# Two key chunks per running-maximum step, and nine chunks of exponentials summed on GpSimd, in an attention and soft-MoE kernel

## The chip, the cores and the metric

The kernel runs on one core of a Trainium2 chip. The metric is the device time of one execution in microseconds (us), as the median of several runs. In what follows PE is TensorE's matrix multiplication, DVE is VectorE, ACT is ScalarE, POOL is GpSimd and SP is the queue of SyncE, which issues the loads and stores.

## The reference

Attention over pooled queries, and a soft mixture of experts on its output. All is float32; the sums over keys below are the part that the change touches.

```python
# q, k, v: (8 batches, 8 heads, 1152, 64); phi: (512, 32); w1: (8, 512, 1024); w2: (8, 1024, 512)
q_pool = q.reshape(B, H, S // 2, 2, D).mean(axis=3)          # 576 queries
scores = scale * np.matmul(q_pool, k.transpose(0, 1, 3, 2))  # 576 x 1152
scores = scores - np.max(scores, axis=-1, keepdims=True)
attn = np.exp(scores)
attn = attn / (np.sum(attn, axis=-1, keepdims=True) + 1e-09)
x = heads side by side of np.matmul(attn, v)                 # (4608, 512)
logits = x @ phi                                             # (4608, 32)
d = softmax of logits over all 4608 rows
slot_input = d.T @ x                                         # 32 slots, 4 for each of 8 experts
slot_out = np.maximum(slot_input[e] @ w1[e], 0) @ w2[e]
return softmax of logits over the 32 slots @ slot_out
```

## The kernel before

The attention is cut into 32 pairs of heads and each pair into three thirds of 192 pooled queries: 96 units, which run one after the other through a pipeline of several units' depth. A unit holds keys on the partitions: nine chunks of 128 keys, each a block of 128 partitions x (2 heads x 192 queries = 384 columns).

What a unit does, under the names that the order and the profile use:

- `S`: PE makes the scores of one or two chunks in a PSUM tile `sc` (two such tiles in turn; five tiles a unit, of chunks 0-1, 2-3, 4-5, 6-7 and 8). `C`: ACT copies the tile to the unit's SBUF buffer `s` (three buffers, so a unit's copy needs what was read of the unit three before). `X`: DVE takes the running maximum over chunks into `M`, reading the scores from PSUM, after ACT has read them.
- `mt`, `mc`, `mb`: PE turns `M` round, DVE reduces over keys, and PE spreads the maximum of each query over the partitions of a PSUM bank `m`. `sub`: DVE subtracts it from `s` in place, three chunks (1152 columns) at a time. `exp`: ACT takes the exponential of three chunks in place.
- `av`: PE multiplies the nine chunks by the values into `U`. `add`: POOL adds chunks up into `cs`. `sums`: PE multiplies `cs`, and what chunk POOL left out, by a matrix of ones, which sums over the keys. `zt`, `rc`, `rr`: DVE, ACT and DVE turn the sums into reciprocals; `xT`: POOL multiplies the unit's result by them. `qs`: POOL adds the query pairs of the next pair of heads, once in three units.

After each batch (12 units) the soft-MoE steps follow (`lg`, `to`, `cb`, `rm`, `nm`, `ex`, `cz`, `on`, `ga` and so on), mixed in among the units of later batches; the expert weights' products form the last 60 us.

Nothing is looped on the chip. `graph` lists all steps with a cost and a due time from the table `K["t"]`, `plan` takes them one by one and picks, on the engine that is free first, the ready step with the lowest due time, and the steps are written in that order. Each engine then runs its own list strictly in order, so a step that waits holds up all behind it on its engine. All engines' instructions go through the helper at L341, so in the profile the groups are told apart by tile names.

The nine chunks' sum is taken in two ways: `adds=(7, 7, 2)` says that POOL adds chunks 0 to 7 into one `cs`, seven additions each of which reads what the last one wrote, and `sums` lets PE take chunk 8 by itself and then `cs`. The last unit has two POOL additions and three on DVE into a tile `c2`. `maxi` makes one instruction for each chunk from 1 on: the first compares chunk 1 in PSUM with chunk 0 in `s`, the others compare a chunk in PSUM with `M`.

Of the kernel before, what the change touches and what calls it, by code (L numbers as in the profile page):

```python
# [9 lines left out]
F32 = mybir.dt.float32  # L10
# [15 lines left out]
    wait=dict(PE=0.086, ACT=0.046, DVE=0.0, Pool=4.872),  # L26
    adds=(7, 7, 2),
# [4 lines left out]
        S=(-419.409, -572.597, -228.216, -358.029, -359.095),  # L32
        C=(-84.784, 269.944, 218.068, -577.589, -79.03),
        X=(-761.046, -254.853, -1002.385, -608.138, -1071.065),
        mt=(-274.632,),
        mc=(-400.52,),
        mb=(-445.98,),
        sub=(-970.04, -736.195, 46.605),
        exp=(-298.507, -391.891, 8.919),
        add=(61.121, 79.596, 138.735, -61.814, 27.096, -118.037, -447.03, 87.051, -331.16),  # L40
        av=(-72.896, -655.1, 1.867, 139.969, 198.999, -251.069, -106.455, 238.404, 113.064),
        sums=(-46.238, -107.59, 249.379, -104.045, -13.513, -134.769, -185.84, -434.517, -83.5, -69.249),
        ue=(-426.57,),
        tc=(-460.765,),
        eps=(13.909,),
        rcp=(38.892,),
        tr=(4.372,),
        ad2=(92.766, -165.96, -728.717, -41.076, -40.387, 11.096, 31.403, 182.215, -386.141),
        nx=(-269.644,),
        ldk=(-344.296,),  # L50
        ldq=(349.768,),
        ldv=(-14.581,),
        qs=(107.426,),
        lg=(-279.404, -0.679, -381.845, 154.224),
        to=(560.808, 859.479, 646.063, 506.384),
        cb=(-186.311, 159.143),
        rm=(512.075, 120.581),
        nm=(-132.399,),
        ex=(-28.039,),
        ns=(400.668,),  # L60
        ce=(-460.62,),
        cz=(-13.045,),
        cm=(-565.973,),
        on=(574.955, 668.981, 964.928, 547.585, 762.85, 285.43, 526.881, 86.153, 107.36, 223.665, 295.103, 920.683),
        we=(-328.071, -289.113),
        ga=(20.378, -479.397, -578.354),
        end_lg=(106.83, -231.5, 354.048, 498.579),
        end_to=(-4.744, 972.49, 123.821, -202.665),
        end_cb=(-233.64, -225.948),
        end_rm=(374.475, 5.169),  # L70
        end_nm=(-356.522,),
        end_ex=(101.789,),
        end_ns=(202.856,),
        end_ce=(17.199,),
        end_cz=(89.883,),
        end_cm=(-72.978,),
        end_on=(262.546, 297.303, 519.604, 283.168, 921.932, -138.51, 416.415, -107.54),
        end_we=(-1262.411, -855.42),
        end_ga=(-16.24, -915.587, 124.689),
        fin_lg=(-453.425, -361.783),  # L80
        fin_to=(184.025, 13.836),
        fin_cb=(89.484, 234.863),
        fin_rm=(1078.782,),
        fin_nm=(-92.156,),
        fin_ex=(447.138,),
        fin_ns=(828.836,),
        fin_ce=(-538.17,),
        fin_cz=(-1160.965,),
        fin_cm=(-294.828,),
        fin_on=(676.225, 510.466, -82.377, 963.76),  # L90
        fin_we=(-453.209, -1047.033),
        fin_ga=(502.969, -358.259, 8.644),
        fin_gs=(-253.634,),
# [19 lines left out]
def pool_t(n):  # L113
    return 0.1 + 0.00241 * n, 0.06 + 0.00241 * n
# [8 lines left out]
def graph(K, B, HP, NT3, Q, NW):  # L123
# [223 lines left out]
def pooled_attention_soft_moe(ctx: ExitStack, tc: tile.TileContext, q, k, v, phi, w1, w2, out):  # L347
# [147 lines left out]
    class Unit:  # L495
# [458 lines left out]
```

## Time and profile before

| what | value |
|---|---|
| median of 3 runs | 993.19 us (992.81 to 994.21) |
| the profiled execution's own time | 993.46 us |
| its span, first to last instruction | 991.7 us |
| mean granted TensorE clock | 0.995 |
| busy share of the span: PE, DVE, POOL, ACT | 97%, 92%, 77%, 76% |
| first and last of the 96 first additions on POOL (`cs<-s`), start | 21.1 us, 916.7 us |

The profile gives, for each engine, the time in which it had an instruction in hand; PE's is modelled, since its matrix products overlap. Two instructions of one engine may overlap in the record by some tens of nanoseconds, so what an instruction costs its engine is read from start to start and not from its own length. The attention takes the span up to about 920 us and the expert products the rest; the argument is about the first.

### The profile page before, as it was taken

How to read it: one execution, taken by the hardware profiler on the slowest of the kernel's cores; microseconds unless marked ns; L12 is line 12 of the kernel's file. 1: busy time of each engine (PE TensorE's matmuls, PEld its weight loads, DVE VectorE, ACT ScalarE, POOL GpSimd, SP SyncE). 2: the span in 40 equal slices, each digit the busy share in tenths (PEclk: the TensorE clock that was granted, in tenths of full speed). 3: DMA queues.
4: the chain of work that ended last, by engine and by line, in shares of the span. 5: the costliest groups of instructions: out<-in, count | busy, mean ns of one | idle time of the engine just before them, and what ended most of it. 6: DMA issues, size and time to landing. Idle time of an engine off the chain costs nothing.

```text
span 991.7 us, 24308 instructions
## 1 busy us (share of the span) xinstructions
PE 958.6 (97%) x9358; PEld 673.0 (68%) x9358; DVE 910.1 (92%) x1595; ACT 753.9 (76%) x1120; POOL 768.4 (77%) x814
## 2 busy tenths in 40 slices
PE   6999999999999999999999999999999999999995
PEld 4666767677767777676677767777677777776542
DVE  5999999999999999999999999999999999999423
ACT  4778888787878788788778878787887888787323
POOL 2888888788888889888888888788897888888200
PEclk9999999999999999999999999999999999999998
DMA  5122322232242322212221211212221211213998
GB/s 170 49 92 94 115 94 94 70 104 82 70 140 70 115 92 73 95 58 104 73 82 63 69 53 52 71 49 73 73 73 52 70 49 54 68 47 131 345 405 351
DMA packets 27683, 101.24 MB, mean 102 GB/s; under 512 B 3504, under 2 KB 4016, under 8 KB 27568
## 3 DMA queue, kind: packets, MB, share of 16 engines
q1 hardware_dynamic: 27568, 99.69, 29.2%
q8 instruction: 74, 1.21, 0.5%
q14 instruction: 41, 0.34, 0.1%
HBM read 90.24 MB, written 9.44 MB: 101 GB/s over the span
## 4 chain that ended last, share of the span: by engine, by line
PE 51%; DVE 30%; issue 11%; ACT 5%; DMA 1%; SPq 0%; POOL 0%; ACTq 0%; DVEq 0%
PE sc L341 18%; DVE M L341 17%; PE U L341 15%; PE m L341 13%; DVE s L341 9%; PE b L341 5%; ACT s L341 5%; DVE rr L341 1%; DMA q<-in_q_dram 1%; DVE rmax L341 1%; DVE mc L341 1%; DVE bm L341 0%; DVE rc L341 0%; PE idle L341 0%; ACT lT L341 0%
## 5 line engine op out<-in xcount | busy, mean ns | idle before, releaser
L341 POOL TENSOR_TENSOR cs<-cs,s 128x384 f32<-128x384 f32 x571 | 573.1, 1004 | 54.7 <-ACT s L341 20.6
L341 ACT COPY s<-sc 128x768 f32<-128x768 f32 (+1 forms) x480 | 342.4, 737 | 145.9 <-PE sc L341 130.5
L341 PE MATMUL sc<-qs,k 64*128 64x192 f32 x3456 | 382.2, 347 | 20.9 <-DVE M L341 8.4
L341 DVE TENSOR_TENSOR s<-s,m 128x1152 f32<-128x1152 f32 x288 | 382.0, 1341 | 6.7 <-PE m L341 5.8
L341 DVE TENSOR_TENSOR M<-sc,M 128x384 f32<-128x384 f32 x672 | 367.7, 547 | 15.5 <-ACT s L341 4.8
L341 PEld LDWEIGHTS sc<-qs,k 64*128 64x128 f32 x3456 | 277.2, 188 | 122.9 <-issue 70.1
L341 PE MATMUL U<-s,v 128*64 128x192 f32 x3456 | 343.3, 331 | 0.2 <-ACT Us L341 0.2
L341 ACT ACTIVATE s<-s 128x1152 f32<-128x1152 f32 x288 | 333.0, 1169 | 13.0 <-DVE s L341 8.5
L341 PEld LDWEIGHTS U<-s,v 128*64 128x64 f32 x3456 | 234.1, 137 | 57.9 <-issue 26.7
L341 POOL TENSOR_TENSOR cs<-s 128x384 f32<-128x384 f32 x96 | 96.5, 1005 | 82.6 <-ACT s L341 81.8
L341 POOL TENSOR_TENSOR xT<-rr,Us 128x192 f32<-128x192 f32 x95 | 56.8, 598 | 2.8 <-DVE rr L341 2.7
L341 DVE TENSOR_TENSOR M<-sc,s 128x384 f32<-128x384 f32 x96 | 51.6, 538 | 5.0 <-ACT s L341 4.8
L341 POOL TENSOR_TENSOR qs<-q 128x576 f32<-128x576 f32 x31 | 44.0, 1419 | 13.9 <-DMA q<-in_q_dram 13.9
L341 DVE TENSOR_REDUCE mc<-m 128x3 f32<-128x384 f32 x96 | 52.4, 546 | 1.2 <-PE m L341 1.1
L341 PE MATMUL m<-ident,M 128*128 128x128 f32 x288 | 52.5, 291 | 0.0
L341 PE MATMUL m<-s,ones 128*64 128x192 f32 x388 | 52.5, 349 | 0.0
L341 PE MATMUL m<-ident,mc 128*128 128x128 f32 x288 | 51.1, 287 | 0.0
L341 PE MATMUL m<-cs,ones 128*64 128x192 f32 x384 | 49.7, 337 | 0.0
L341 PEld LDWEIGHTS m<-ident,M 128*128 128x128 f32 x288 | 29.8, 141 | 23.1 <-issue 22.8
L341 PEld LDWEIGHTS m<-ident,mc 128*128 128x128 f32 x288 | 29.9, 136 | 19.9 <-issue 12.2
L341 DVE STREAM_TRANSPOSE zt<-m 128x192 f32<-128x192 f32 x96 | 35.8, 373 | 1.1 <-PE m L341 1.1
L341 DVE STREAM_TRANSPOSE rr<-rc 128x192 f32<-128x192 f32 x96 | 35.4, 368 | 0.3
(90 smaller groups left out, 449.0 us busy)
## 6 DMA issues: line engine op xcount, KB each, us to landing
w<-in_moe_w_dram SPq DMA_DIRECT2D x64, 512.0 KB, 5.9
v<-in_v_dram SPq DMA_DIRECT2D x32, 576.0 KB, 3.8
k<-in_k_dram SPq DMA_DIRECT2D x31, 576.0 KB, 3.8
q<-in_q_dram SPq DMA_DIRECT2D x31, 576.0 KB, 3.8
out_dram<-ob SPq DMA_DIRECT2D x24, 384.0 KB, 4.2
q<-in_q_dram SPq DMA_DIRECT2D x1, 384.0 KB, 7.2
k<-in_k_dram SPq DMA_DIRECT2D x1, 320.0 KB, 5.7
k<-in_k_dram SPq DMA_DIRECT2D x1, 256.0 KB, 3.1
```

The lines of the kernel that those rows point to most:

```text
L341: return self.tc.keep_in_program_order(op(*args, **kwargs))
```

## The change

1. **Maximum over two chunks at a time.** `M` becomes two blocks of 384 columns. `X` of the tile of chunks 2-3 compares both with chunks 0-1 in `s` (768 columns, one instruction), the tiles 4-5 and 6-7 compare with `M` in the same way, a new step `Xf` (method `fold`) takes the maximum of the two blocks of `M`, both in SBUF, and chunk 8 is compared with the result. The tile of chunks 0-1 is no longer read by DVE. `M` has one buffer of twice the size in place of two.
2. **All nine chunks summed on POOL.** Eight additions in two sums: `cs` takes chunks 0, 1, 4, 6, 8, and chunk 2 takes 3, 5, 7 in place; the eighth addition puts chunk 2 onto `cs`. PE's `sums` has `cs` alone, in all but the last unit.
3. **Three small DVE instructions** that had a constant as operand (`nm`, the addition in `cz`, the addition before `zs`) get a second tensor in SBUF in its place.
4. **A new table of due times,** some step costs, and a term `stay` in `plan`, which favours a PE step that uses PE in the same mode (rows, columns or the full array) as the one before.

```diff
-    adds=(7, 7, 2),
+    stay=287.389,
+    adds=(8, 8, 2),
...
-        X=(-761.046, -254.853, -1002.385, -608.138, -1071.065),
+        X=(-718.744, -1124.601, -586.904, -1071.804, 795.214),
+        Xf=(-611.616,),
...
-        return ("add", u, max(c, 1)) if max(c, 1) <= adds[u] else ("sums", u, NC if c == 0 else c)
+        return ("add", u, (1, 1, 8, 2, 3, 4, 5, 6, 7)[c])
...
+        for i in range(1, na + 1):
+            if i == 1:
+                d = [("exp", u, 0), old(u > 1, "sums", u - 2, NC)]
+            elif na == 8:
+                d = [("add", u, i - 1 if i == 8 else max(i - 2, 1))] + [("add", u, 6) if i == 8 else ("exp", u, group_of[i + 1])]
+                d += [("av", u, 2)] if i == 2 else []
+            else:
+                d = [("add", u, i - 1), ("exp", u, group_of[i])]
...
-            k = min((k for k in ks if when[k] <= t0 + K["wait"].get(e, 0.0) + 1e-9), key=lambda k: (ops[k][2], at[k]))
+            k = min((k for k in ks if when[k] <= t0 + K["wait"].get(e, 0.0) + 1e-9),
+                    key=lambda k: (ops[k][2] - (K["stay"] if ops[k][7] == last and ops[k][7] else 0.0), at[k]))
...
         def maxi(self, i):
-            for x, c in enumerate(TI[i]):
-                if c:
-                    M = self.M
-                    if M is None:
-                        self.M = un.tile([P, 2, QU], F32, name=f"M{self.u}", tag="M")
-                        M = self.s[:, 0]
-                    dve.tensor_tensor(self.M, self.ps[i][:, :, x * QU:(x + 1) * QU], M, op=ALU.max)
+            if i == 1:
+                self.M = un.tile([P, 2, 2, QU], F32, name=f"M{self.u}", tag="M", bufs=1)
+            n = len(TI[i])
+            ps = self.ps[i][:, :, :n * QU].rearrange("p h (c q) -> p c h q", c=n)
+            if n == 2:
+                dve.tensor_tensor(self.M, ps, self.s[:, 0:2] if i == 1 else self.M, op=ALU.max)
+            else:
+                dve.tensor_tensor(self.M[:, 0], ps[:, 0], self.M[:, 0], op=ALU.max)
+
+        def fold(self):
+            dve.tensor_tensor(self.M[:, 0], self.M[:, 0], self.M[:, 1], op=ALU.max)
...
-        def add(self, c):
-            sv = self.s[:, c]
-            if c == 1:
+        def add(self, i):
+
+            s = self.s
+            if i == 1:
                 self.cs = un.tile([P, 2, QU], F32, name=f"cs{self.u}", tag="cs")
-            pool.tensor_tensor(self.cs, self.s[:, 0] if c == 1 else self.cs, sv, op=ALU.add)
+            if i == 1:
+                t = self.cs, s[:, 0], s[:, 1]
+            elif self.u == NU3 * B * HP - 1:
+                t = self.cs, self.cs, s[:, i]
+            elif i == 8:
+                t = self.cs, self.cs, s[:, 2]
+            elif i % 2:
+                t = self.cs, self.cs, s[:, i + 1]
+            else:
+                t = s[:, 2], s[:, 2], s[:, i + 1]
+            pool.tensor_tensor(*t, op=ALU.add)
...
-            dve.tensor_scalar(self.nm, new, -1.0, None, op0=ALU.mult)
+            dve.tensor_tensor(self.nm, zero, new, op=ALU.subtract)
...
-            dve.tensor_scalar(self.cz, self.cz, EPS, None, op0=ALU.add)
+            dve.tensor_tensor(self.cz, self.cz, eps[:NQ].to_broadcast([NQ, self.nt]), op=ALU.add)
...
-        dve.tensor_scalar(zs, rsum, EPS, None, op0=ALU.add)
+        dve.tensor_tensor(zs, rsum, eps, op=ALU.add)
```

What the new order does is shown at two places in the middle of the program. First DVE before, from the first maximum of unit 46 to its last (a row names the engine's operation, the tile written and the tiles read; the number behind a letter is the unit or buffer, and x2 stands for two alike in a row):

```order
L341 TENSOR_TENSOR M46_4497<-sc0_136,s1_139 128x384
L341 TENSOR_REDUCE mc45_4502<-m2_135 128x3
L341 TENSOR_TENSOR M46_4497<-sc1_137,M46_4497 128x384 x2
L341 TENSOR_TENSOR s0_138<-s0_138,m2_135 128x1152 x2
L341 TENSOR_TENSOR M46_4497<-sc0_136,M46_4497 128x384 x2
L341 STREAM_TRANSPOSE zt44_4559<-m0_133 128x192
L341 TENSOR_TENSOR M46_4497<-sc1_137,M46_4497 128x384 x2
L341 STREAM_TRANSPOSE rr43_4571<-rc43_4483 128x192
L341 RECIPROCAL rc44_4565<-rc44_4565 128x6
L341 TENSOR_TENSOR M46_4497<-sc0_136,M46_4497 128x384
```

Eight instructions write `M46`, six of them in pairs in which the second reads what the first wrote; `zt` and `rr` of units two and three back stand between them. The same stretch of DVE after the change, at unit 49:

```order
L350 TENSOR_TENSOR M49_4594<-sc0_138,s1_141 128x768
L350 TENSOR_TENSOR s0_140<-s0_140,m0_135 128x1152
L350 TENSOR_TENSOR M49_4594<-sc1_139,M49_4594 128x768
L350 TENSOR_TENSOR s0_140<-s0_140,m0_135 128x1152
L350 TENSOR_TENSOR M49_4594<-sc0_138,M49_4594 128x768
L350 STREAM_TRANSPOSE zt46_4650<-m2_137 128x192
L350 TENSOR_TENSOR M49_4594<-M49_4594 128x384
L350 RECIPROCAL rc46_4659<-rc46_4659 128x6
L350 TENSOR_TENSOR M49_4594<-sc1_139,M49_4594 128x384
L350 STREAM_TRANSPOSE rr46_4670<-rc46_4659 128x192
```

Five instructions write `M49`, no two of them next to each other; the fourth is the fold, which reads no PSUM. `zt` is now that of the unit three back. POOL before, over the additions of unit 46 and the first of unit 47:

```order
L341 TENSOR_TENSOR cs46_4649<-s1_139 128x384
L341 TENSOR_TENSOR cs46_4649<-cs46_4649,s1_139 128x384 x5
L341 TENSOR_TENSOR xT3_3837<-rr45_4718,Us45_4711 128x192
L341 TENSOR_TENSOR cs46_4649<-cs46_4649,s1_139 128x384
L341 TENSOR_TENSOR cs47_4745<-s2_140 128x384
```

There are seven additions in one chain, broken once by `xT`. POOL after the change, over the additions of unit 45 and the first of unit 46:

```order
L350 TENSOR_TENSOR cs45_4416<-s0_140 128x384
L350 TENSOR_TENSOR cs45_4416<-cs45_4416,s0_140 128x384 x2
L350 TENSOR_TENSOR s0_140<-s0_140 128x384 x2
L350 TENSOR_TENSOR cs45_4416<-cs45_4416,s0_140 128x384
L350 TENSOR_TENSOR s0_140<-s0_140 128x384
L350 TENSOR_TENSOR cs45_4416<-cs45_4416,s0_140 128x384
L350 TENSOR_TENSOR xT3_3738<-rr44_4486,Us44_4422 128x192
L350 TENSOR_TENSOR cs46_4503<-s1_141 128x384
```

There are eight additions, and the two sums take turns, in most units without a break but for the last two: over the whole program 2.5 additions a unit directly follow one that they depend on (125 `cs` behind the same `cs`, 32 chunk-2 sums behind the same sum, 80 last additions behind the chunk-2 sum that they read, over 96 units).

More of the change, by code (lines that the diff above doesn't have):

```diff
@@ L25 @@
     bufs=3,
-    wait=dict(PE=0.086, ACT=0.046, DVE=0.0, Pool=4.872),
-    adds=(7, 7, 2),
+    stay=287.389,
+    wait=dict(PE=0.226, ACT=0.162, DVE=0.177, Pool=0.222),
+    adds=(8, 8, 2),
     more=3,
@@ new lines @@
+        Xf=(-611.616,),
+        mt=(-723.921,),
+        mc=(-114.844,),
+        mb=(-258.845,),
+        sub=(-619.663, -102.814, 1329.497),
+        exp=(-642.998, 884.145, 2721.12),
+        add=(-198.042, 1322.564, -125.887, -190.614, 154.697, -76.997, 1064.624, 181.041, -383.843),
+        av=(-131.033, -285.378, 7.096, -154.967, -134.833, 1122.981, 753.574, 1255.771, 50.287),
+        sums=(248.993, -468.15, 1008.625, -343.84, -281.108, -244.636, -433.554, 1772.701, -715.422, 357.278),
@@ new lines @@
+        ue=(219.326,),
+        tc=(-619.755,),
+        eps=(-475.199,),
+        rcp=(587.085,),
+        tr=(1037.822,),
+        ad2=(-53.911, -555.751, -604.838, -526.867, 730.457, -438.819, -56.242, -328.898, -440.675),
+        nx=(-394.76,),
+        ldk=(1741.983,),
+        ldq=(-545.242,),
+        ldv=(-712.945,),
+        qs=(1280.303,),
+        lg=(444.851, 1827.585, 1378.479, 269.315),
+        to=(-352.527, -351.216, 595.522, -21.759),
+        cb=(-404.16, -621.947),
+        rm=(-593.4, -101.797),
@@ new lines @@
+        nm=(1924.0,),
+        ex=(868.118,),
+        ns=(1829.478,),
+        ce=(-122.558,),
+        cz=(2775.066,),
+        cm=(1393.56,),
+        on=(-454.454, -58.618, 1350.106, -112.696, 801.818, -835.286, 715.879, 207.384, 682.139, 1275.364,
+            -383.737, 661.371),
+        we=(-597.411, 350.652),
+        ga=(1799.669, -165.502, -420.515),
+        end_lg=(-98.197, -419.284, -79.663, -540.569),
+        end_to=(-608.902, -43.815, 408.079, 74.295),
+        end_cb=(513.126, -242.586),
@@ new lines @@
+        end_rm=(-231.148, 1919.33),
+        end_nm=(-65.218,),
+        end_ex=(-95.024,),
+        end_ns=(-432.945,),
+        end_ce=(-436.159,),
+        end_cz=(438.218,),
+        end_cm=(-559.666,),
+        end_on=(18.047, 1709.155, 1820.299, 6.308, 1328.871, -126.235, -611.963, 497.934),
+        end_we=(-367.952, -647.455),
+        end_ga=(-134.148, -375.889, -728.043),
+        fin_lg=(305.033, 82.614),
+        fin_to=(236.995, -870.323),
+        fin_cb=(236.963, -750.654),
+        fin_rm=(-13.239,),
@@ L94 @@
+        fin_nm=(-865.594,),
+        fin_ex=(-154.868,),
+        fin_ns=(478.151,),
+        fin_ce=(16.679,),
+        fin_cz=(1089.035,),
+        fin_cm=(-70.505,),
+        fin_on=(-1089.827, -542.03, 2626.542, 835.695),
+        fin_we=(-352.114, 782.849),
+        fin_ga=(-127.911, -315.564, -577.207),
+        fin_gs=(-350.135,),
     ),
@@ L187, in graph @@
             op(("C", u, i), "ACT", act_t(2 * Q * len(tl)), d)
-            m = sum(1 for c in tl if c)
-            if m:
-                d = [("C", u, i)] + ([("X", u, i - 1)] if i and (i > 1 or len(TI[0]) > 1) else [])
-                d += [old(u > 1, "mt", u - 2)] if c - m < 1 else []
-                t = dve_t(2 * Q)
-                op(("X", u, i), "DVE", (m * t[0], (m - 1) * t[0] + t[1]), d)
+            if i:
+                before = ("X", u, i - 1) if 1 < i < len(TI) - 1 else ("C", u, 0) if i == 1 else ("Xf", u)
+                op(("X", u, i), "DVE", dve_t(2 * Q * len(tl)), [("C", u, i), before] + [old(u and i == 1, "mt", u - 1)])
+            if i == len(TI) - 2:
+                op(("Xf", u), "DVE", dve_t(2 * Q), [("X", u, i)])
         b = ("m", u)
         op(("mt", u), "PE", 0.33, [("X", u, len(TI) - 1)], b, take=True)
-        op(("mc", u), "DVE", (0.485, 0.56), [("mt", u), old(u > 1, "mb", u - 2)], b)
+        op(("mc", u), "DVE", (0.465, 0.55), [("mt", u), old(u > 1, "mb", u - 2)], b)
         op(("mb", u), "PE", 0.34, [("mc", u)], b)
@@ L379, in pooled_attention_soft_moe @@
     nc.gpsimd.memset(eps, EPS)
+    zero = const.tile([P, 1], F32, name="zero")
+    nc.gpsimd.memset(zero, 0.0)
     ones = const.tile([P, D], F32, name="ones")
```

90 lines of the change are left out of this document (15 added, 75 removed).

## Prediction

> **What bounds the kernel now.** I read the page's busy shares, then one window of 770 us from the steady middle, then the groups of instructions in it, and last the timelines of DVE and POOL, for what one instruction costs from start to start.
>
> ```profile
> span 991.7 us, 24308 instructions
> core 0: us, PE busy (x) PEld busy (x) DVE busy (x) ACT busy (x) POOL busy (x), PEclk, DMA share, GB/s
> 110.00:880.00 770.00, 761.94 (x7440) 544.83 (x7438) 750.54 (x1294) 621.24 (x913) 653.00 (x685) 1.00 0.24 77
> L341 POOL TENSOR_TENSOR cs<-s x96: 990/1005/1017, 21.1 to 916.7; 128x384 f32<-128x384 f32 x96
> PE 51%; DVE 30%; issue 11%; ACT 5%; DMA 1%; SPq 0%; POOL 0%; ACTq 0%; DVEq 0%
> ```
>
> The first additions of units 0 and 95 start 895.6 us apart, so a unit takes 895.6 / 95 = 9.43 us. DVE is busy in 750.5 of 770 us, which is 9.19 us of each unit: it is the bound. PE looks as full, and half of the chain of waits is PE's, but its busy time is modelled and holds gaps like these:
>
> ```profile
> PEld m L341 <- issue: 62.8, 265, 0.5
> PEld sc L341 <- issue: 55.9, 206, 0.8
> PEld U L341 <- issue: 22.8, 115, 0.5
> 441.60 0.55 PE L341 MATMUL m<-s,ones 128*64 128x192 f32 x4
> ```
>
> In that window PE's weight loads stood idle for 141 us without a named cause, mostly where PE goes from one kind of product to another. I take PE as second, with slack. POOL's 653 us leave out the pauses inside its chains, which the next part adds.
>
> **Cost on DVE.** Before, a unit has eight maxima: two alone and three pairs.
>
> ```profile
> 447.75 0.54 DVE L341 TENSOR_TENSOR M<-sc,s 128x384 f32<-128x384 f32 x1
> 448.22 0.54 DVE L341 TENSOR_REDUCE mc<-m 128x3 f32<-128x384 f32 x1
> ...
> 451.44 1.14 DVE L341 TENSOR_TENSOR M<-sc,M 128x384 f32<-128x384 f32 x2
> 452.50 1.34 DVE L341 TENSOR_TENSOR s<-s,m 128x1152 f32<-128x1152 f32 x1
> 453.76 0.74 DVE L341 SCALAR_TENSOR_TENSOR slot<-slot,corr,m 96x512 f32<-96x512 f32 x1
> ```
>
> One alone takes 448.22 - 447.75 = 0.47 us, a pair 452.50 - 451.44 = 1.06 us, since its second waits for the first's result. A unit pays 2 x 0.47 + 3 x 1.06 = 4.12 us. The subtraction of 1152 columns takes 453.76 - 452.50 = 1.26 us, so 384 columns more cost (1.26 - 0.47) / 2 = 0.40 us, and a maximum over 768 columns, which no row has, about 0.87 us. (Its bounds are the pair's 1.06 and the 0.79 that the columns alone cost; I take the line through both lengths.) After: 3 x 0.87 + 0.47 for chunk 8 + a fold of 0.47 = 3.55 us. Clean, DVE saves 0.57 us a unit and falls to 8.62.
>
> But the fold reads two tensors in SBUF, as no other large instruction of the steady part does; the maxima and subtractions have one operand in PSUM. The trace has that form at the end, and small ones at each batch:
>
> ```profile
> 917.83 1.00 POOL L341 TENSOR_TENSOR cs<-cs,s 128x384 f32<-128x384 f32 x1
> 918.21 1.04 DVE L341 TENSOR_TENSOR c<-s 128x384 f32<-128x384 f32 x1
> 919.28 1.22 DVE L341 TENSOR_TENSOR c<-c,s 128x384 f32<-128x384 f32 x2
> 174.81 1.00 POOL L341 TENSOR_TENSOR cs<-cs,s 128x384 f32<-128x384 f32 x1
> 174.83 1.00 DVE L341 TENSOR_TENSOR rmax<-bm 128x1 f32<-128x1 f32 x1
> L341 DVE SCALAR_TENSOR_TENSOR rmax<-bm,rmax x7: 219/986/994, 288.5 to 925.6; 128x1 f32<-128x1 f32 x7
> L341 DVE SCALAR_TENSOR_TENSOR rsum<-rsum,corr,bs x8: 175/178/216, 308.5 to 931.3; 128x1 f32<-128x1 f32 x8
> L341 DVE TENSOR_SCALAR nm<-rmax x9: 153/154/155, 175.9 to 927.8; 128x1 f32<-128x1 f32 x9
> L341 DVE TENSOR_SCALAR cz<-cz x9: 164/166/169, 181.7 to 929.9; 96x6 f32<-96x6 f32 x7, 96x4 f32<-96x4 f32 x1, 96x2 f32<-96x2 f32 x1
> L341 DVE TENSOR_TENSOR M<-sc,M x672: 511/552/560, 8.5 to 911.0; 128x384 f32<-128x384 f32 x168
> ```
>
> The exact shape of the fold took 1.04 us beside a POOL addition and 0.56 without. It ended at 919.25, 0.42 us after POOL's addition ended at 918.83, and 384 columns cost 0.40 us: it did nothing until POOL was done. `rmax`, one column wide, took 0.99 us beside an addition of 1.00. `M`, with one operand in PSUM, never took over 0.56 us, though POOL was nearly always busy. So the fold costs what is left of POOL's instruction plus 0.42 us. POOL starts an addition about every 0.96 us (next part); if the fold meets it anywhere, 0.48 us are left on average, and the fold takes 0.90 us, that is 0.34 more than 0.56. Its bounds are 0.56 and 0.96 + 0.42 = 1.38 us.
>
> The new `nm` and the addition in `cz` have two SBUF inputs too. `nm` stands right behind `rmax`, when POOL has just begun its next addition: 0.15 becomes about 1.0 us as in `rmax`; `cz` gains about half an addition, 0.45. That is 1.3 us in 12 units, 0.11 each (bounds 0 and 0.16). The edit before `zs` runs once and can wait for one POOL instruction, 1.0 us at most, which I leave to the range. DVE: 9.19 - 0.57 + 0.34 + 0.11 = 9.07 us a unit.
>
> **Cost on POOL.**
>
> ```profile
> 441.48 1.01 POOL L341 TENSOR_TENSOR cs<-cs,s 128x384 f32<-128x384 f32 x1
> 442.44 1.42 POOL L341 TENSOR_TENSOR qs<-q 128x576 f32<-128x576 f32 x1
> 443.82 1.01 POOL L341 TENSOR_TENSOR cs<-s 128x384 f32<-128x384 f32 x1
> 444.90 1.00 POOL L341 TENSOR_TENSOR cs<-cs,s 128x384 f32<-128x384 f32 x1
> 445.88 0.59 POOL L341 TENSOR_TENSOR xT<-rr,Us 128x192 f32<-128x192 f32 x1
> 446.43 4.25 POOL L341 TENSOR_TENSOR cs<-cs,s 128x384 f32<-128x384 f32 x4
> 450.65 0.59 POOL L341 TENSOR_TENSOR xT<-rr,Us 128x192 f32<-128x192 f32 x1
> L341 POOL TENSOR_TENSOR cN<-cN,cz 96x192 f32<-96x192 f32 x7 | 3.5, 507 | 2.4 <-DVE cz L341 2.4
> ```
>
> An addition followed by something independent takes 442.44 - 441.48 = 0.96 us, one followed by an addition that reads its result 444.90 - 443.82 = 1.08: 0.12 for each dependent step. `qs` takes 1.38, a third of it, 0.46, on each unit; `xT` 0.55; `cN` 0.5 in 12 units, 0.04. Before: 7 x 0.96 + 4.9 dependent steps x 0.12 + 0.55 + 0.46 + 0.04 = 8.36 us, and POOL waits for the rest of 9.43. After: 8 x 0.96 + 2.5 x 0.12 + 0.55 + 0.46 + 0.04 = 9.03. The ninth chunk costs POOL 0.67 us, and it is nearly full.
>
> Then comes the fold seen from POOL. No row shows a POOL instruction behind a long DVE instruction of this form. Its bounds are 0, if POOL goes on beside it, and 0.56 us, the fold's whole length; I take 0.42, the time for which the fold ran alone after POOL's end. That gives 9.03 + 0.42 = 9.45 us a unit, 0.02 more than now. POOL becomes the bound.
>
> The Trainium skill, "SBUF — State Buffer", section "SBUF: two separate sides", states that a VectorE instruction with two SBUF inputs and a GpSimd instruction that reads SBUF hold their shared port pair exclusively for the whole instruction, and that the loser fully blocks. The rows of `c<-s` and `rmax` agree for VectorE as the loser; no row here shows GpSimd as the loser. Read literally, with the whole 0.56 us, it would make POOL 9.59 us a unit, an estimate.
>
> **What else moves.** PE loses one product with ones (four instructions, 0.55 us with its change of mode), and the new order changes PE's mode 64 times less; both fall on an engine with slack, and if POOL and DVE cover it, they bring nothing. The tile of chunks 0-1 is freed one maximum earlier and `M` has one buffer, not two: the first maximum of a unit must wait until PE has turned the last unit's `M`, but `mc` of that unit stands before it on DVE anyway. The in-place sum makes a unit's second tile copy wait for the eighth addition of three units before; that is over 14 us after its exponentials begin (two units of 9.4 less some 4.5 us for the first subtraction and exponential), and POOL needs 9.5, so POOL may lag 5 us before ACT waits. SP's list is the same but for some neighbours exchanged. The expert part at the end stays as it is.
>
> **The sum.** POOL's work sets the date of the last unit:
>
> ```profile
> 21.13 1.01 POOL L341 TENSOR_TENSOR cs<-s 128x384 f32<-128x384 f32 x1 [4.04 <-ACT s L341]
> 30.86 1.01 POOL L341 TENSOR_TENSOR cs<-s 128x384 f32<-128x384 f32 x1 [2.25 <-ACT s L341]
> ```
>
> From 21.1 us, 95 units at 9.45 and about 2 us in which POOL still waits for its second unit make 920.9 us, against 916.7: 4.2 us later. The last steps follow it as now. The profiled execution took 993.46 us, 1.8 more than its span and 0.3 more than the median of 993.19; so 993.5 + 4.2 = 997.7, as a median about 998 us. With the fold's price on POOL at 0.38 it would be 994, at 0.56 about 1011.
>
> **Rivals.** First, POOL is not held up, or for a short time only, since its own start-up runs under the fold. DVE's 9.07 us with today's idle 0.24, and POOL's 9.03, then give 9.25 to 9.31 us a unit, some 12 to 17 us less: about 978. For it speaks that no row shows POOL waiting; it decides as soon as POOL's loss is under 0.25 us a fold. Second, the folds mostly miss POOL's additions, or read without waiting: DVE at 8.62, POOL at 9.03, a unit near 9.15, 27 us less: 966. For it speaks `rsum`, whose two tensors lie in SBUF as well and which took 0.18 us at all eight batches: it came in a pause of POOL. Against it: every `rmax` and `c` that began beside a running POOL instruction waited, and with POOL nearly full there are few pauses. Third, the two effects cancel within 0.2%: POOL's loss is 0.35 to 0.4 us. Fourth, it is worse: POOL's loss is the whole 0.56, or its lag reaches `zt`, which waits in DVE's list for the sums; 1006 and more.
>
> **Chances.** About 0.2%, some 2 us, is what a measurement here can tell from no change. POOL-bound and slower, 995.2 to 1006: 0.37, the likeliest, predicted at 998. Worse than that: 0.09. Within 0.2%: 0.15. First rival, 970 to 991: 0.27; second, 955 to 970: 0.12. So faster 0.39, same 0.15, slower 0.46. The likeliest case's own range is 995 to 1006; to hold 8 in 10 with both signs I give 964 to 1009, which leaves out part of the second rival and of the worst case.
>
> **What would show it.** In the profile after: `M<-sc,M` of 768 columns near 0.94 us long; the fold `M<-M` near 0.9 us on average and seldom 0.55; POOL's start-to-start of independent additions 0.96 us, with longer ones, near 1.4, where a fold ran; POOL's waits for `exp` gone and DVE's idle grown to some 0.4 us a unit; `nm` near 1.0 us. If POOL still waits for ACT, or its additions beside a fold are no longer than others, the first rival holds. If the folds take 0.55 us, the second does.

## The result, and the profile after

| | before | after |
|---|---|---|
| median | 993.34 us (992.81 to 994.21, 4 runs) | 1017.58 us (1016.49 to 1019.08, 4 runs) |
| ratio | | 1.0244 (95%: 1.0226 to 1.0262) |
| profiled execution, its span | 993.46, 991.7 us | 1016.49, 1014.5 us |
| granted TensorE clock | 0.995 | 0.994 |

The changed kernel is 2.4% slower. The direction was forecast, the size was not: 1017.6 lies above the range. Two rows of the page after, the span and the shares of the chain of waits; then the window of 770 us (the columns are those of the row of before), the first additions on POOL, and what PE waited for in that window (in all, times, longest):

```profile
span 1014.5 us, 23218 instructions
...
DVE 36%; PE 26%; POOL 19%; ACT 9%; issue 9%; DMA 0%; SPq 0%; ACTq 0%; POOLq 0%; DVEq 0%
```

```profile
110.00:880.00 770.00, 723.60 (x6932) 512.83 (x6930) 747.75 (x1020) 608.91 (x889) 724.70 (x746) 1.00 0.23 75
```

```profile
L350 POOL TENSOR_TENSOR cs<-s x96: 989/1006/1330, 19.2 to 942.7; 128x384 f32<-128x384 f32 x96
```

```profile
PE sc L350 <- DVE M L350: 41.9, 61, 1.4
...
PEld sc L350 <- DVE M L350: 35.1, 83, 1.6
```

The first additions are (942.7 - 19.2) / 95 = 9.72 us apart, 9.43 before. DVE is busy in 747.75 of 770 us, as full as before, which is now 9.44 us a unit in place of 9.19: DVE still has the least slack of the two, and a unit asks more of it. POOL's 724.7 us are 9.15 a unit, and it idles more. PE now waits 77 us for maxima ahead of its score products; in the same window of before it was 1.1 us. Most of this wait is not the loss: 58 us of it stay (32.1 and 25.9) in the kernel "at the fold's place" of the table below, which is faster than before. The groups on DVE (busy, mean ns | idle just before), first of after, then one of before:

```profile
L350 DVE TENSOR_TENSOR M<-sc,M 128x768 f32<-128x768 f32 x159 | 150.7, 948 | 0.1
L350 DVE TENSOR_TENSOR M<-sc,s 128x768 f32<-128x768 f32 x79 | 75.3, 954 | 1.4
L350 DVE TENSOR_TENSOR M<-M 128x384 f32<-128x384 f32 x79 | 72.3, 915 | 0.4
L350 DVE TENSOR_TENSOR nm<-zero,rmax 128x1 f32<-128x1 f32 x6 | 5.6, 927 | 0.2
```

```profile
L341 DVE TENSOR_TENSOR M<-sc,M 128x384 f32<-128x384 f32 x569 | 311.2, 547 | 12.7 <-ACT s L341 3.7
```

The maximum over 768 columns is 0.95 us long and the fold 0.915, both near the prediction's 0.94 and 0.9. A ledger by unit is needed for the rest. For 72 units in the middle I add up, on DVE and on POOL, each instruction's own time (from its start to the next one's start, less the idle time between) and the idle time; the two make the period.

| kernel (names below) | time, us | period | DVE own | DVE idle | POOL own | POOL idle | the join, own |
|---|---|---|---|---|---|---|---|
| before | 993.3 | 9.48 | 9.24 | 0.24 | 8.02 | 1.45 | none |
| after | 1017.6 | 9.75 | 9.47 | 0.28 | 9.16 | 0.59 | 0.84 |
| no fold | 983.0 | 9.40 | 8.63 | 0.77 | 8.87 | 0.54 | none |
| fold as a reduction | 1019.9 | 9.73 | 9.49 | 0.25 | 8.91 | 0.82 | 0.84 |
| POOL nearly idle | 972.4 | 9.25 | 8.99 | 0.26 | 3.05 | 6.21 | 0.46 |
| join in chunk 8's tile, behind `rc` (small ones undone) | 1017.8 | 9.72 | 9.12 | 0.60 | 8.90 | 0.82 | 0.54 |
| join in chunk 8's tile, at the fold's place | 988.3 | 9.40 | 9.08 | 0.32 | 8.87 | 0.52 | 0.46 |
| the same, small ones undone | 976.3 | 9.26 | 8.99 | 0.28 | 8.88 | 0.38 | 0.47 |

Times are in us a unit but for the first column; "join" is whatever brings the two blocks of `M` together, and the experiments below say what each kernel leaves out. One execution of the last kernel took 1775 us, for no known reason; its ratio leaves that one out, and without it the median is 976.24.

### The profile page after: what moved, and what is told of

It is laid out like the page before. It is cut to its first block, busy times and chain, and to the rows that moved or that the text cites. A ratio compares the mean times of both kernels' runs of the same rounds, so it can differ in the third digit from the quotient of the medians.

```text
span 1014.5 us, 23218 instructions
## 1 busy us (share of the span) xinstructions
PE 933.1 (92%) x8978; PEld 648.9 (64%) x8978; DVE 930.7 (92%) x1307; ACT 757.1 (75%) x1120; POOL 875.9 (86%) x910
## 3 DMA queue, kind: packets, MB, share of 16 engines
HBM read 90.24 MB, written 9.44 MB: 98 GB/s over the span
## 4 chain that ended last, share of the span: by engine, by line
DVE 36%; PE 26%; POOL 19%; ACT 9%; issue 9%; DMA 0%; SPq 0%; ACTq 0%; POOLq 0%; DVEq 0%
DVE M L350 21%; POOL cs L350 11%; PE sc L350 10%; ACT s L350 9%; DVE s L350 8%; POOL s L350 8%; PE m L350 7%; PE b L350 5%; PE U L350 4%; DVE mc L350 2%; DVE zt L350 1%; DVE cz L350 1%; DVE nm L350 1%; POOL xT L350 1%; DVE rmax L350 1%
## 5 line engine op out<-in xcount | busy, mean ns | idle before, releaser
L350 PE MATMUL sc<-qs,k 64*128 64x192 f32 x3456 | 392.7, 349 | 63.2 <-DVE M L350 55.8
L350 POOL TENSOR_TENSOR cs<-cs,s 128x384 f32<-128x384 f32 x381 | 392.9, 1031 | 25.8 <-ACT s L350 11.1
L350 PEld LDWEIGHTS sc<-qs,k 64*128 64x128 f32 x3456 | 273.1, 186 | 165.8 <-DVE M L350 52.7
L350 ACT ACTIVATE s<-s 128x1152 f32<-128x1152 f32 x288 | 337.5, 1172 | 51.7 <-DVE s L350 51.5
L350 PE MATMUL U<-s,v 128*64 128x192 f32 x3456 | 326.9, 331 | 0.5 <-ACT Us L350 0.3
L350 POOL TENSOR_TENSOR s<-s 128x384 f32<-128x384 f32 x285 | 301.5, 1058 | 12.5 <-PE U L350 8.6
L350 DVE TENSOR_TENSOR M<-sc,M 128x768 f32<-128x768 f32 (+1 forms) x288 | 235.2, 817 | 1.0 <-ACT s L350 0.5
L350 DVE TENSOR_TENSOR M<-sc,s 128x768 f32<-128x768 f32 x96 | 91.5, 954 | 6.1 <-ACT s L350 4.4
L350 DVE TENSOR_TENSOR M<-M 128x384 f32<-128x384 f32 x96 | 87.3, 910 | 0.7
L350 PEld LDWEIGHTS m<-ident,mc 128*128 128x128 f32 x288 | 29.3, 136 | 20.9 <-DVE mc L350 19.1
L350 ACT COPY Us<-U 128x192 f32<-128x192 f32 x96 | 31.3, 326 | 13.9 <-POOL xT L350 12.7
```

What stands on the lines that cost most here:

```text
L350: return self.tc.keep_in_program_order(op(*args, **kwargs))
```

## The experiments

Each is an edit to the changed kernel, unless it says that it starts from the kernel before. Ratios are to the kernel before, run beside it on the same chip (its median lay between 993.66 and 994.38), with their 95% interval. The first theories were A, that waits between DVE and POOL for SBUF cost the time, and B, that POOL's nine chunks, the order or score tiles held too long do.

**The small instructions alone.** First undone in the changed kernel, then put alone into the kernel before:

```diff
-            dve.tensor_tensor(self.nm, zero, new, op=ALU.subtract)
+            dve.tensor_scalar(self.nm, new, -1.0, None, op0=ALU.mult)
```

(and in the same way `cz` and `zs`).

> The changed kernel with its three small DVE edits undone (nm, the addition in cz and the one before zs have constants again); the rest and the order are the same. Theory A, waits at the shared SBUF port enter the period, since DVE and POOL are both within 5% of it: in the changed kernel nm takes 0.93 us and the cz addition 0.79 where they took 0.15 and 0.17, 1.4 us a batch with rsum's share more; they stand in the chain from the batch's maximum, so 8 batches give 11 to 14 us: 1004 to 1007. Theory B, POOL with its nine chunks is the bound and DVE has slack: under 3 us, 1015 to 1018.

> The kernel before with the three small edits of the change alone. Theory A: DVE is the bound there (97.5% busy), so 1.4 us a batch gives 11 to 14 us: 1004 to 1007. Theory B: the waits fall into times when the batch's steps have slack, under 3 us: 993 to 996.

Undone: 1008.1 us, 1.0140 (1.0124 to 1.0157), 9.5 less than the change and a little above A's range. Put alone into the kernel before: 1013.1, 1.0194 (1.0163 to 1.0224), which is 19 us more and beyond what was expected. There `nm` stands beside POOL's longest instruction, at every batch (the timeline, and below it the row of the waits for `nm`, in all, times, longest):

```profile
407.48 1.32 DVE L341 TENSOR_TENSOR nm<-zero,rmax 128x1 f32<-128x1 f32 x1
407.39 1.40 POOL L341 TENSOR_TENSOR qs<-q 128x576 f32<-128x576 f32 x1
```

```profile
ACT corr L341 <- DVE nm L341: 14.9, 6, 2.5
```

One column takes 1.32 us in place of 0.15. ACT waits 14.9 us for `nm` in six batches (7.8 before), and what stands behind `corr` on ACT waits with it. Part of the excess comes with a lower clock. ACT's `lT` stands behind `corr`, and PE waits 1.86 us for it where it waited 0.7 at most before; the 28 products that follow take 3.77 us in place of 2.44 (the row of before, then two of this run):

```profile
405.96 2.44 PE L341 MATMUL U<-s,v 128*64 128x192 f32 x28
410.01 0.60 PE L341 MATMUL sc<-qs,k 64*128 64x192 f32 x4 [1.86 <-ACT lT L341]
411.62 3.77 PE L341 MATMUL U<-s,v 128*64 128x192 f32 x28
```

The granted clock is 0.98 in this window of 110 us, from 330 to 440, and in three more of the seven from 110 to 880; it was 1.00 in all seven before. From unit 12 on, by the starts of first additions twelve units apart, a batch is 1.1 to 1.2 us longer than before where the clock stayed at 1.00, about what A counted, and 2.8 to 2.9 where it did not. Why it fell at some batches and not at others, no run shows.

So the small ones matter. In the changed kernel they are 9.5 of its 24 us, the smaller part.

**No fold.** The step issues nothing; the maximum leaves out chunks 3, 5 and 7 (and with the second edit the small ones are undone too).

```diff
-            dve.tensor_tensor(self.M[:, 0], self.M[:, 0], self.M[:, 1], op=ALU.max)
+            pass
```

> The changed kernel without the fold: the maximum over the second block of M (chunks 1, 3, 5, 7) is left out, everything else and the order are the same. Theory A: DVE loses 0.84 us a unit and POOL the 0.33 us by which an addition beside a fold is longer; DVE's own work is then 8.5 and POOL's 9.0 of the 9.75 us period, which should fall to 9.2 to 9.4: 965 to 985. Theory B (the fold's lock matters only through POOL, the 0.4 us a unit of mutual waiting stays as it comes from the order): 9.4 a unit, 984 to 990. If the fold is not the cause: 1010 or more.

> The changed kernel without the fold (so the maximum leaves out chunks 3, 5 and 7) and with the three small DVE instructions as before: the changed kernel with no DVE instruction of the steady part that has two operands in SBUF. Theory A: the 9.5 us that the small instructions cost beside the fold come off the 983.0 without the fold as well: 971 to 976. Theory B (the small instructions only mattered because the fold had used up the slack): 980 to 984.

983.0 us, 0.9881 (0.9859 to 0.9903), within A's range, and 969.7, 0.9761 (0.9745 to 0.9778), a little below it. Without the fold, the nine chunks on POOL and the new order are faster than before: B falls as far as POOL and the order as such are meant.

**The join in the tile of chunks 6-7.** Two ways. In the first the second block is put into the PSUM tile, and the fold reads the tile; the next unit's scores had to be made to wait for it, so the planner wrote another order. In the second the order is the change's and three maxima stand in a row.

```diff
+            if i == len(TI) - 2:
+                dve.tensor_tensor(ps[:, 1], ps[:, 1], self.M[:, 1], op=ALU.max)
+                dve.tensor_tensor(self.M[:, 0], ps[:, 0], self.M[:, 0], op=ALU.max)
+                dve.tensor_tensor(self.M[:, 0], ps[:, 1], self.M[:, 0], op=ALU.max)   # second way
```

> The changed kernel computing all, but with the fold reading one operand from PSUM: the tile of chunks 6-7 is compared in two instructions, the second block's result written back into that PSUM tile, and the fold compares this with the first block in SBUF; the next unit's first score tile waits for the fold. Theory A: DVE takes three times 0.47 where it took 0.87 + 0.84, 0.30 less a unit, and POOL 0.33 less; 9.0 each, the period 9.3 to 9.4: 973 to 985. Theory B: POOL's 0.33 alone comes out, 9.4 a unit, 984 to 990; if the later release of the PSUM tile holds PE up, 0.3 a unit of it goes back, about 1010.

> The changed kernel in its own order, fold in SBUF taken out; the two blocks are brought together inside the PSUM tile of chunks 6-7 by three maxima of 384 columns. Nothing is left out of the result. Theory A: the maxima cost 3.74 us a unit on DVE in place of the 3.95 measured, POOL gets its 0.33 us a unit back: 0.2 to 0.33 us x 96 = 20 to 32 us less than 1017.6, so 986 to 998. Theory B (what counts is the new order and that PE waits for score tiles): the tile of chunks 6-7 is held as long or longer, 1012 to 1022.

1041.0 us, 1.0462 (1.0432 to 1.0492), and 1044.9, 1.0513 (1.0491 to 1.0534): A's and B's expectations failed both times. In the second, the three maxima stand ahead of `zt`:

```profile
434.58 0.56 DVE L350 TENSOR_TENSOR sc<-sc,M 128x384 f32<-128x384 f32 x1
435.18 1.15 DVE L350 TENSOR_TENSOR M<-sc,M 128x384 f32<-128x384 f32 x2
436.25 0.37 DVE L350 STREAM_TRANSPOSE zt<-m 128x192 f32<-128x192 f32 x1
436.99 0.19 DVE L350 RECIPROCAL rc<-rc 128x6 f32<-128x6 f32 x1 [0.37 <-ACT rc L350]
436.65 0.30 ACT L350 ACTIVATE rc<-zt,eps 128x6 f32<-128x6 f32 x1 [0.67 <-DVE zt L350]
```

`zt` comes late, ACT stands 0.67 us for it, then DVE 0.37 for ACT, and behind ACT's `rc` stand the copies of the next scores. That was the hint that the place in DVE's queue counts.

**The two-chunk maximum in the kernel before**, with its seven chained additions, its order and its small instructions: with three maxima in the tile of chunks 6-7; with the fold in SBUF ahead of chunk 8's maximum; with the join in chunk 8's tile (two maxima, `sc8 = max(sc8, M1)`, `M0 = max(sc8, M0)`); and with no join (chunks 1, 3, 5, 7 left out).

> The kernel before, in its own order, with its seven chained additions and its small instructions, but with the maximum over two chunks at a time (768 columns), where the two blocks are brought together inside the PSUM tile of chunks 6-7: three maxima of 384 columns, each with one operand in PSUM, so that no maximum reads two tensors in SBUF. Theory A (waits between DVE and POOL for SBUF cost the time, the two-chunk maximum itself saves): DVE needs 2 x 0.87 + 1.53 + 0.47 = 3.74 us a unit for the maxima in place of 4.12, POOL is as before with 1.4 us of slack; 0.38 x 96 = 36 us can be gained as far as PE lets it: 957 to 975, faster than the kernel before. Theory B (the two-chunk maximum hurts because it keeps a score tile longer from PE, whatever the SBUF waits): 990 to 1010.

> As the kernel before with the two-chunk maximum, but with the fold of the change: both operands in SBUF, right ahead of the maximum over chunk 8. Seven chained additions on POOL, old order, old small instructions. Theory A: the fold lasts 0.90 and one POOL addition in each unit 0.33 longer; DVE saves 4.12 - (3 x 0.87 + 0.90 + 0.47) = 0.14 to 0.24 us a unit, and POOL, at 8.0 + 0.33 of 9.5 us, has room for its loss: 970 to 985, that is 5 to 20 us behind the kernel with the fold in PSUM, and far from the 1017 of the whole change, because there POOL has no slack. Theory B (the fold as such costs what the change lost): 1000 or more.

> The kernel before, in its own order, with the two-chunk maximum; the two blocks come together in the PSUM tile of chunk 8, by two maxima of 384 columns, behind `zt` in the order and not ahead of it as in the version with three maxima in the tile of chunks 6-7 (1017). Maxima: 3 x 0.87 + 1.06 = 3.67 us a unit in place of 4.09. Theory E (the version with three maxima lost because they stood ahead of `zt`, on which ACT and the next unit's scores wait): 960 to 985, faster than before. Theory F (the old order cannot use the two-chunk maximum, since its copies and subtractions wait at other places as well): 995 to 1015.

> The kernel before, in its own order, with the two-chunk maximum and nothing that brings the blocks together (the maximum leaves out chunks 1, 3, 5 and 7). DVE needs 4.13 - 3.08 = 1.05 us a unit less, and nothing else changes. If DVE alone bounds the kernel before: 900 to 950, as far as PE lets it. Theory F (the old order has no room: what the units wait for is the path from one engine to the next, which does not get shorter): 975 to 1000.

1017.3 (1.0242, 1.0226 to 1.0257), 1042.7 (1.0491, 1.0476 to 1.0507), 1018.1 (1.0241, 1.0222 to 1.0261) and 976.6 us (0.9824, 0.9809 to 0.9838). The second came out as B said and the last as F; the first and the third lie a little above what the slower of their theories gave. Three things follow. Without a join, DVE's own work falls by 0.75 us a unit and the period by only 0.16; the rest becomes idle time (0.83): DVE alone did not bound the kernel before, the path from engine to engine did so as well. None of the three places that were tried in the old order covers a join: against the 976.6 without one it costs 40.7, 66.1 and 41.5 us. And ahead of chunk 8's maximum the fold in SBUF costs 24.6 more than the join in PSUM, although POOL idles 1.7 us a unit in that kernel: whoever pays for the wait, it is not POOL for want of time.

**Two that went astray.** The old kernel with only the nine-chunk sum on POOL, and the version with the join in chunk 8's tile planned anew with the old table of due times:

> The kernel before, in its own order, with its maximum chunk by chunk and its small instructions, but with all nine chunks added up on POOL in two sums (the steps stay where the seven additions stood; the last of them issues three), and PE without chunk 8's sum. POOL gets 0.96 us a unit more: 8.02 + 0.96 = 8.98 of 9.47 us, and PE 0.32 less. Theory A (the waits between DVE and POOL made the change slow, not POOL's additions): 985 to 1000. Theory B (nine chunks are too much for POOL, whose sums come too late): 1005 to 1030.

> The version with the two-chunk maximum and the blocks brought together in the tile of chunk 8, old POOL part, old small instructions, old table of due times, but planned anew with the new steps' costs and with what they wait for (the version in the old order took 1018.1). Theory E (the old order was the obstacle): 960 to 990, faster than before. Theory F (the score tiles held longer are, whatever the order): 1000 to 1025.

1132.6 us, 1.1383 (1.1346 to 1.1419), and 1073.5, 1.0797 (1.0779 to 1.0815). In the first the old order puts the sum into chunk 2 ahead of PE's product with that chunk, so its result is another one, and PE waits 197 us for `cs`, whose last three additions are issued where one stood; it says nothing on nine chunks, though the time lies beyond both expectations. In the second the old due times do not fit the new steps: DVE idles 1.30 us a unit, and the time lies beyond both expectations as well. It says nothing on the two-chunk maximum.

**The fold with one operand.** `M` is laid element beside element, and one reduction reads 768 elements. Nothing is left out.

```diff
-            dve.tensor_tensor(self.M[:, 0], self.M[:, 0], self.M[:, 1], op=ALU.max)
+            dve.tensor_reduce(self.M0, self.M, axis=AX.X, op=ALU.max)   # M: [P, h, q, 2 blocks]
```

> The changed kernel with the fold as a reduction with one operand: the two blocks of M lie element beside element, and one reduction over 768 elements brings them together at the fold's place in the order. Nothing is left out. It should last about 0.85 us (the maximum over 768 columns took 0.87), close to the 0.91 that the fold lasted with its wait, but it need not wait for POOL, nor POOL for it; the small instructions still do. Theory C (what costs is that POOL is held up and the two engines wait for each other in turns): POOL's additions go back from 1.31 to about 0.98 us beside the fold, 0.33 us a unit, 985 to 1003. Theory D (what costs is only the time that DVE spends at that place of its queue): 1010 to 1020, as the change.

> The same with the three small instructions as before, so that no instruction of the steady part on DVE has two operands in SBUF, with nothing left out. To be held against the changed kernel with the small ones undone (1008.1). Theory C: 970 to 990. Theory D: 1002 to 1010.

1019.9 us, 1.0254 (1.0230 to 1.0278), and with the small ones undone 1008.3, 1.0139 (1.0123 to 1.0155): the same as the fold (1017.6 and 1008.1), as theory D said. This is the run that settles who pays. By the ledger the reduction has the fold's own time, 0.84 us, and POOL gets its loss back (8.91 in place of 9.16); the time does not move. The other layout of `M` leaves the two-chunk maxima at their price (0.90 and 0.88 us own time, against 0.89 and 0.87). POOL also leaves the chain of waits, of which it was 19% after:

```profile
DVE 41%; PE 37%; ACT 11%; issue 6%; POOL 4%; DMA 0%; ACTq 0%; SPq 0%; DVEq 0%; POOLq 0%
```

So POOL being held up costs nothing here; DVE's 0.84 us at that place do.

**POOL nearly idle.** Of the eight additions of a unit only the first and the last are issued (the sums leave out chunks 3 to 8); DVE's instructions and order are the change's.

```diff
+            if 1 < i < 8 and self.u < NU3 * B * HP - 1:
+                return
```

> The changed kernel, the same instructions on DVE in the same order, but of the eight additions on POOL only the first and the last in each unit (the sums leave out chunks 3 to 8). The fold then meets a POOL instruction in about 30% of the cases: it should last about 0.47 + 0.3 x 0.4 = 0.6 us in place of 0.91, and the small instructions mostly 0.1 to 0.2. Theory D (what counts is the time that DVE spends, and of each microsecond saved there some 0.4 reaches the span, as taking the whole fold away showed: 34.6 us for 0.84 x 96 = 81): 0.25 x 96 x 0.43 = 10 us for the fold and 5 to 9 for the small ones, 998 to 1003. Theory G (POOL's eight additions themselves hold up the rest, through late sums and score buffers that come free late): 965 to 985.

972.4 us, 0.9782 (0.9768 to 0.9797), far less than theory D gave, and within theory G's range, though not by its mechanism: DVE's own time falls by 0.47 us a unit and the period by 0.50, and the last experiment, with the small ones undone, comes within 4 us of this time with all of POOL's additions in place. The fold takes 0.52 us (median), and it lies in a hole. A unit in the middle without the fold, then after, then with POOL nearly idle:

```profile
405.46 0.96 DVE L350 TENSOR_TENSOR M<-sc,M 128x768 f32<-128x768 f32 x1
406.34 0.37 DVE L350 STREAM_TRANSPOSE zt<-m 128x192 f32<-128x192 f32 x1
407.10 0.19 DVE L350 RECIPROCAL rc<-rc 128x6 f32<-128x6 f32 x1 [0.39 <-ACT rc L350]
...
407.93 1.32 DVE L350 TENSOR_TENSOR s<-s,m 128x1152 f32<-128x1152 f32 x1
```

```profile
421.18 0.95 DVE L350 TENSOR_TENSOR M<-sc,M 128x768 f32<-128x768 f32 x1
422.05 0.37 DVE L350 STREAM_TRANSPOSE zt<-m 128x192 f32<-128x192 f32 x1
422.35 0.99 DVE L350 TENSOR_TENSOR M<-M 128x384 f32<-128x384 f32 x1
423.26 0.18 DVE L350 RECIPROCAL rc<-rc 128x6 f32<-128x6 f32 x1
...
424.13 1.31 DVE L350 TENSOR_TENSOR s<-s,m 128x1152 f32<-128x1152 f32 x1
421.92 1.00 POOL L350 TENSOR_TENSOR s<-s 128x384 f32<-128x384 f32 x1
422.87 1.32 POOL L350 TENSOR_TENSOR cs<-cs,s 128x384 f32<-128x384 f32 x1
```

```profile
404.47 0.96 DVE L350 TENSOR_TENSOR M<-sc,M 128x768 f32<-128x768 f32 x1
405.64 0.52 DVE L350 TENSOR_TENSOR M<-M 128x384 f32<-128x384 f32 x1
406.10 0.19 DVE L350 RECIPROCAL rc<-rc 128x6 f32<-128x6 f32 x1
...
406.95 1.32 DVE L350 TENSOR_TENSOR s<-s,m 128x1152 f32<-128x1152 f32 x1
```

DVE's `rc` needs ACT's `rc`, which needs `zt`; without a fold DVE stands still for 0.39 us between them. From the maximum over chunks 6-7 to the last subtraction pass 407.93 - 405.46 = 2.47 us without a fold, 406.95 - 404.47 = 2.48 with a fold that does not wait, and 424.13 - 421.18 = 2.95 with one that does. In this unit the fold itself is free and its wait is paid in full. It stands right between `zt` and `rc` in 69 of the 96 units.

**The join in chunk 8's tile, behind `rc` and at the fold's place.** The two maxima that had cost 41.5 us in the old order, put into the new one (small ones undone), then only moved: the first of them goes to where the fold stood, between `zt` and `rc`, since ACT has copied chunk 8's tile by then. Nothing is left out, and nothing else changes.

```diff
         def fold(self):
-            dve.tensor_tensor(self.M[:, 0], self.M[:, 0], self.M[:, 1], op=ALU.max)
+            if self.copied:
+                self.join()
+
+        def join(self):
+            ps = self.ps[len(TI) - 1][:, :, :QU]
+            dve.tensor_tensor(ps, ps, self.M[:, 1], op=ALU.max)
...
```

(`copied` says that ACT's copy of chunk 8's tile has been issued; the lines that keep these marks stand where the dots are. Chunk 8's maximum, unchanged, then takes both along; in the version behind `rc` the join stands right ahead of it and `fold` is empty.)

> The changed kernel with the small instructions as before and the two blocks brought together in the PSUM tile of chunk 8 (two maxima of 384 columns there, no step Xf). Nothing is left out, and nothing of the steady part on DVE has two operands in SBUF. Maxima: 0.89 + 1.75 + 1.06 = 3.70 us a unit in place of 3.95 (with the small ones undone: 1008.1 us). Theory D: 0.25 x 96 x 0.43 to 1 = 10 to 24 us less, 984 to 998. Theory H (the score tile of chunk 8, held 0.5 us longer, holds PE up): 1005 to 1020.

> The changed kernel, its order and its POOL part, the small instructions as in the change; only the fold is another: at its place, between zt and rc, the second block of M goes into the PSUM tile of chunk 8 (384 columns, one operand in PSUM), and the maximum over chunk 8 takes both along. Nothing is left out, and there is one instruction of the same width where the fold stood. Theory A' (the fold's wait for POOL, 0.84 in place of 0.47 us in a gap of 0.39 us between zt and rc, made the change slow): 0.37 x 96 = 36 us less than 1017.6, 978 to 988, faster than before. Theory H (a score tile that is written and read once more holds PE up): 1005 to 1020.

> The same with the three small instructions as before the change, so that no instruction of the steady part on DVE that the change brought has two operands in SBUF. Theory A': another 9 us less, 968 to 978, as the version with POOL nearly idle (972.4), with nothing left out. Theory H: 996 to 1010.

Behind `rc`: 1017.8 us, 1.0237 (1.0221 to 1.0252), which is in theory H's range. At the fold's place with the change's small instructions: 988.3 (987.17 to 995.13, 7 runs), 0.9962 (0.9937 to 0.9988), at the upper end of A'; its longer runs have the lower granted clock, 0.983 in the longest against 0.990 in the shortest. With the small ones undone: 976.3 (975.98 to 976.30 in the three runs that count), 0.9818 (0.9797 to 0.9840), within A'. H falls with it, since the score tile is written and read once more there too. The same unit there, and behind `rc`:

```profile
405.08 0.96 DVE L350 TENSOR_TENSOR M<-sc,M 128x768 f32<-128x768 f32 x1
405.95 0.37 DVE L350 STREAM_TRANSPOSE zt<-m 128x192 f32<-128x192 f32 x1
406.25 0.54 DVE L350 TENSOR_TENSOR sc<-sc,M 128x384 f32<-128x384 f32 x1
406.71 0.19 DVE L350 RECIPROCAL rc<-rc 128x6 f32<-128x6 f32 x1
...
407.58 1.31 DVE L350 TENSOR_TENSOR s<-s,m 128x1152 f32<-128x1152 f32 x1
405.46 1.02 POOL L350 TENSOR_TENSOR s<-s 128x384 f32<-128x384 f32 x1
```

```profile
425.05 0.19 DVE L350 RECIPROCAL rc<-rc 128x6 f32<-128x6 f32 x1 [0.39 <-ACT rc L350]
425.16 0.54 DVE L350 TENSOR_TENSOR sc<-sc,M 128x384 f32<-128x384 f32 x1
```

POOL's addition runs on beside the join, from 405.46 to 406.48, and neither waits. The same instruction one place further back in DVE's queue leaves the hole of 0.39 us open, adds itself behind it, and makes 41.5 us. With the small ones undone, the version at the fold's place beats the kernel before by 1.8% and, set against the 1017.6 of the first comparison, the changed one by 4.1%, with the reference's whole computation. It is 6.6 us above the kernel that brings nothing together (969.7): the join in the hole is nearly free, not quite. The 29.3 us gained at the fold are 0.31 us a unit, and the 12.0 from the small ones 0.13.

## Why the prediction was wrong

**What came as predicted.** DVE full before, though it was not the only bound (the kernel before with no join); 0.87 us for 768 columns (own time 0.87 to 0.89); the fold's price, 0.90 predicted and 0.91 measured. It ended 0.416 us (median) after the POOL instruction that it met, predicted 0.42. `nm` took 0.93 us, predicted about 1.0. POOL's side of the wait, for which the prediction had no row, exists too: 90 of its 762 additions lasted over 1.1 us, 1.28 on average, where the median is 1.007.

**The step that failed: "POOL becomes the bound".** The sum was made of POOL's 9.03 + 0.42 = 9.45 us a unit. POOL's own time came out at 9.16, since it lost 0.25 a unit and not 0.42, and it still idled 0.59. The fold as a reduction gave POOL its loss back and left the time where it was. So the first rival's condition, POOL not held up, was met there, and the result was 1020 and not 978. That the kernel came out slower, as the likeliest case said, is therefore luck as far as that case's mechanism goes. The time lies in the fourth rival's range, 1006 and more, but not for its reasons: POOL's loss was not the whole 0.56 us, and DVE did not stand idle ahead of `zt` in the middle units. The prediction's own sign for the first rival, that POOL still waits, was there; what put the time 40 us above that rival is the next step.

**The step under it: DVE at 9.07 us a unit.** Measured the same way it is 9.44. By the ledger, 0.14 of the 0.37 is that I took 4.12 us of maxima, measured from start to start, out of 9.19 us of busy time, in which they are 3.98: most of it is the pauses inside the pairs (the 12.7 us of idle in the row of before, less the 3.7 spent waiting for ACT, are 0.11 in each of 81 units), which lie in the first number and not in the second. The new maxima and fold cost 3.95 and not 3.89 (0.06), the small ones 0.13 and not 0.11. Another 0.12 are subtractions, `mc` and `rc` (0.14, less 0.02 that `rr` got shorter), which in the new order are more often followed by something that must wait, and lose an overlap of 0.08 us each time. Together these make 0.34. So DVE had no slack in which 0.34 us of waiting could vanish; I had given it 0.38. These parts are worked out, not tested one by one.

**The term that decides.** I priced the fold's wait rightly and then let it fall on an engine with room. In the order it stands, in most units, in a hole of 0.39 us, in which the fold alone is nearly free and its wait is not: 0.84 less 0.47 of own time, 0.37 us a unit, 36 us over 96 units. Taking POOL's additions away, which removes this wait and those of `nm` (0.16 us there), gave 45 us. Removing the wait at the fold, DVE's and with it POOL's, gave 29.

**The small instructions** at 0.11 us a unit were nearly right in the new order (9.5 and 12.0 us over 96 units, 0.10 and 0.13) and too small for the old one (19 us, 0.20), where `nm` meets a longer POOL instruction, the wait goes on to ACT and PE, and the clock falls at some batches.

**The second rival**, folds that miss POOL, was priced at 966; with no wait at the fold and POOL at full work it is 976, with POOL nearly idle 972. The price was near, its condition was not met: 13 of 96 folds took under 0.6 us.

**Who is held up.** The Trainium skill, "SBUF — State Buffer", section "SBUF: two separate sides", says that the loser of the shared port pair fully blocks. The trace agrees for VectorE (0.416 us after POOL's end) and now for GpSimd as the loser (the row of 1.32 us beside the fold, 0.85 us of it after the fold's end). What POOL lost there is 0.31 us and not the fold's whole length. The estimate of 1011 us went through POOL; the reduction shows that the time does not come that way.

**Still open** is in part why the wait's removal brought 29 us and not 36. In the middle the period fell by 0.35 us, 34 us over 96 units. In the profiles the 23 units outside the middle gain only 0.27 each, the first addition starts 2.0 us later, and what follows the last unit's first addition is 0.9 longer; why, no run shows.

## What to carry to other kernels

Here two engines held each other up, and only DVE's wait cost time; how much went by the place in DVE's queue where it stood. Look in the trace for the hole that an instruction is to fill, and compare the hole with the instruction's length with the wait. One operand in PSUM, in a tile that is in use anyway, took the fold's wait away at the same width and the same place, and turned 2.4% slower into 0.4% faster; with the three small instructions undone it is 1.8%. And do not subtract times from start to start from busy times: the pauses between dependent instructions are in one and not in the other.

## What was not expected of the hardware

Having only one tensor in SBUF to read was not always enough to be free of POOL. With the small ones undone, the addition of a constant in `cz`, 6 columns, lasts 0.49 us beside POOL, ending with POOL's addition, where it took 0.166 us before (it began there 0.11 us ahead of the end of POOL's addition); `nm`, one column, takes 0.15 beside the same addition:

```profile
194.06 0.15 DVE L350 TENSOR_SCALAR nm<-rmax 128x1 f32<-128x1 f32 x1
194.50 0.49 DVE L350 TENSOR_SCALAR cz<-cz 96x6 f32<-96x6 f32 x1
193.97 1.00 POOL L350 TENSOR_TENSOR cs<-s 128x384 f32<-128x384 f32 x1
```

It does so at all seven batches in the steady part. The same section of the Trainium skill says that a VectorE instruction in a two-port performance mode takes the port pair as well, which would fit `cz` and not `nm`; no run here shows which mode they ran in. The reduction of 768 elements with one operand did not wait: 0.84 us of own time at the fold's place, with POOL's additions beside it at their usual length. And a maximum that is written back into its PSUM tile costs what the others cost, 0.46 us from start to start.
